# Half-filled products of w1's last 64 rows, in pairs on the two row halves of TensorE

## The chip, the cores and the metric

The kernel runs on one core of a Trainium2 chip. The metric is device time in microseconds for one launch, from the start to the end of the program on that core. A change of about 0.5% (6 us) can be told from no change.

## What is computed

A dynamic convolution feeds a two-level mixture of experts. For each of 23040 tokens (8 sequences of 2880) with 192 channels in 8 heads, seven softmax weights mix the token and the six before it. The result goes to one of 16 experts: the best of 4 groups, then the best of 4 experts in that group.

```python
w = softmax(weight_gen)                     # 8 heads, 7 taps a token
x = sum_k w[..., k] * x_shifted[k]          # 192 channels
g = argmax(x @ w_group); e = argmax(x @ w_expert[g])
h = maximum(x @ w1[g, e], 0)                # 192 -> 1024
out = p(g) * p(e) * (h @ w2[g, e])          # 1024 -> 192
```

All inputs and the output are fp32.

## The kernel before

**Stages.** VectorE computes the convolution for 15 groups of tokens, each group 12 tokens for each of the 128 partitions, in two chunks of 6. TensorE transposes and scores a group (`logits`, with `score` on four tiles of 32 columns, line 375). VectorE ranks the tokens (`ranks`) and writes a list of row numbers (`posi`, line 489), and GpSimd scatters the group's twelve columns of rows by it into `rows` in DRAM, sorted by expert (`scatter_row`, line 503). After certain groups `table` makes a table of the blocks of rows that are full. Such a set of blocks is a round. Round 5 takes the tokens up to group 6.

**Visits.** A visit takes one block of 128, 256 or 384 tokens of one expert through both products. The order of the visits is fixed by `ROUNDS`: round 0 has ten visits of 128, rounds 1 to 11 have 4, 5, 7, 5, 7, 5, 6, 7, 5, 4 and 5 visits of 256 (round 10 starts with one of 384), and rounds 12 and 13 the rest. In this text visit k is the k-th, from 0, of those behind the ten short ones, so visit 9 is the first of round 3 and visit 21 the first of round 5. For rounds below 12, and short blocks, w2 is used in whole fp32 (`whole`), and these are the whole visits.

**First product (`gemm1`, line 907).** A whole visit of 256 has four units `u` of two 128-column tiles `v` of w1. The fp32 values are split in two parts each. `wa[:, 0]` and `wa[:, 1]` are the high and the low part of w1's first 128 rows. `wa[:, 2]` holds the high part of its last 64 rows on partitions 0 to 63, and their low part (`w1lo`) on 64 to 127. `xh` and `xl` are the high and low part of the tokens, with the last 64 channels standing on both halves. Five products of 128x256 make one column tile:

```python
terms = ((wa[:, 0, :], xh[:, 0, :]), (wa[:, 1, :], xh[:, 0, :]), (wa[:, 0, :], xl[:, 0, :]), (wa[:, 2, :], xh[:, 1, :]), (wa[:, 2, :], xl[:, 1, :]))
```

In the fifth only the high half of the weights counts; the other half multiplies low part by low part. The result stands in one of three banks `ph0` to `ph2`, taken in turn; ScalarE applies the Relu (line 913).

**Second product (`gemm2`, line 945).** It runs two units behind the first, adds up the eight tiles into `py0` and `py1`, one bank for each 128 tokens, and ScalarE copies them to `y` (line 954, `finish`), from which GpSimd stores them by token number (line 962, `send`). The tokens of a visit are loaded by SyncE (line 779, `xb`), copied by ScalarE (`xd`, line 865), and transposed on TensorE (`tpx`, lines 881 and 882) behind the second unit of the visit before; VectorE makes `xl` from it (line 840, through `delay`).

**Order.** TensorE, ScalarE, VectorE and SyncE execute in the order in which the code is written by a planner: `run` adds up assumed costs for each engine in `clk`, and `fill` puts front work (convolution, softmax, ranking, tables) on VectorE until its clock reaches TensorE's. `gemm1` of a whole unit counts 1.09 us, `gemm2` 1.28. `pump` writes the loads. GpSimd's order is chosen by the compiler. A load of a round's tokens waits for the scatters of all groups up to that round's last.

## Time and profile before

| | us |
|---|---|
| median of three timed runs | 1199.54 (1197.88 to 1202.95) |
| profiled execution, its own time | 1193.24 |
| its span | 1191.6 |
| TensorE busy in it | 1132.8 |
| VectorE busy in it | 959.7 |

The profile is one execution of its own; differences are worked out against its 1193.24 and then moved to the median. Start times in the timelines are microseconds from the start of the span. Lengths of products on TensorE are modelled and overlap, so the distance from one start to the next is what a product takes in a row.

### The profile page before, as it was taken

What the parts mean: (1) busy time and instruction counts of PE and PEld (TensorE: products, weight loads), DVE (VectorE), ACT (ScalarE), POOL (GpSimd) and SP (SyncE); (2) the same over time, 40 slices, a digit from 0 to 9 for tenths busy, and PEclk for the clock granted to TensorE, in tenths of its full rate; (3) what the DMA queues carried; (4) which work ended last, traced back from release to release, by engine and by line L of the source; (5) the groups of instructions that cost most, each with busy time, mean ns of one, the idle gap of its engine ahead of it and who ended that gap; (6) DMA issues with size and microseconds to landing.
All of it is one profiled execution on the core that took longest, in us unless ns stands there. A gap on an engine that the chain in (4) does not pass through costs nothing.

```text
span 1191.6 us, 24474 instructions
## 1 busy us (share of the span) xinstructions
PE 1132.8 (95%) x8357; PEld 1073.7 (90%) x8357; DVE 959.7 (81%) x1646; ACT 651.2 (55%) x1235; POOL 569.1 (48%) x608
## 2 busy tenths in 40 slices
PE   5787899999999999999999999999999989999998
PEld 3444788999999999999999999999899989999997
DVE  8899898999998999899999999898535756666661
ACT  1331345565565655655655655655556766666572
POOL 6154183756273747575656555374664112222211
PEclk9997999999999999999999999999999999999999
DMA  5698799887888877888687878558688675555562
GB/s 172 212 308 224 264 303 308 267 266 249 255 253 261 282 221 239 274 253 264 211 298 228 281 223 293 186 160 257 203 271 256 217 196 159 160 161 159 164 200 76
DMA packets 82758, 275.08 MB, mean 231 GB/s; under 512 B 15063, under 2 KB 31734, under 8 KB 80832
## 3 DMA queue, kind: packets, MB, share of 16 engines
q1 hardware_dynamic: 62296, 229.76, 61.9%
q0 software_dynamic: 20208, 43.39, 11.5%
q8 instruction: 67, 1.10, 0.4%
q14 instruction: 67, 0.55, 0.2%
q10 hardware_dynamic: 120, 0.28, 0.1%
HBM read 225.83 MB, written 48.42 MB: 230 GB/s over the span
## 4 chain that ended last, share of the span: by engine, by line
PE 58%; issue 20%; DVE 7%; DMA 6%; POOL 5%; SPq 2%; ACT 1%; POOLq 1%; DVEq 0%; ACTq 0%
PE py L945 26%; PE ph L907 24%; POOL out L962 4%; DVE pr L294 3%; PE pl L375 2%; DMA raw<-w1lo 1%; PE tpx L882 1%; DMA out<-y,xb 1%; PE tpx L881 1%; DMA wt<-in_weight_gen 1%; DMA w1lo<-raw 1%; DMA xb<-rows 1%; PE ph L335 1%; PE tp L392 1%; POOLq L557 1%
## 5 line engine op out<-in xcount | busy, mean ns | idle before, releaser
L907 PE MATMUL ph<-xh,wa 128*128 128x256 f32 (+1 forms) x1992 | 465.5, 307 | 0.0
L962 POOL DMA_INDIRECT out<-y,xb x189 | 204.9, 1084 | 438.7 <-DVE y L960 193.8
L945 PE MATMUL py<-wc,hh 128*128 128x192 f32 x2160 | 399.9, 326 | 2.1 <-ACT y L954 2.1
L907 PE MATMUL ph<-xl,wa 128*128 128x256 f32 (+1 forms) x1328 | 360.2, 290 | 0.3 <-DVE xl L840 0.3
L945 PEld LDWEIGHTS py<-wc,hh 128*128 128x128 f32 x2160 | 346.4, 190 | 2.4 <-ACT y L954 2.3
L907 PEld LDWEIGHTS ph<-xh,wa 128*128 128x128 f32 x1992 | 337.5, 190 | 3.3 <-issue 1.8
L913 ACT ACTIVATE hh<-ph 128x512 f32<-128x512 f32 (+2 forms) x296 | 165.5, 559 | 262.0 <-PE ph L907 261.8
L294 DVE TENSOR_TENSOR pr<-xin,wt 128x1152 f32<-128x1152 f32 x186 | 248.9, 1350 | 5.5 <-PE py L335 3.5
L907 PEld LDWEIGHTS ph<-xl,wa 128*128 128x128 f32 x1328 | 251.9, 190 | 0.6 <-DVE xl L840 0.6
L503 POOL DMA_INDIRECT rows<-xrow,ix x156 | 227.4, 1457 | 49.4 <-POOL ix L502 35.8
L312 DVE TENSOR_TENSOR xrow<-xrow,pr 128x1152 f32<-128x1152 f32 x144 | 194.6, 1351 | 0.7
L840 DVE SCALAR_TENSOR_TENSOR pr<-ph,hh 128x384 fp32r<-128x384 f32 (+1 forms) x128 | 77.5, 606 | 99.8 <-ACT hh L918 98.6
L840 DVE TENSOR_TENSOR wa<-raw,wa 128x1024 fp32r<-128x1024 f32 x83 | 101.4, 1222 | 31.1 <-ACT wa L816 30.9
L947 PE MATMUL py<-wc,hh 128*128 128x384 f32 x352 | 110.6, 362 | 0.0
L918 ACT ACTIVATE hh<-ph 128x384 fp32r<-128x384 f32 (+1 forms) x128 | 68.4, 534 | 69.8 <-PE ph L907 69.8
L502 POOL COPY ix<-posi 128x1 int32<-128x1 int32 x156 | 70.0, 458 | 63.7 <-DMA rows<-xrow,ix 36.2
L816 ACT CAST wa<-raw 128x1024 fp32r<-128x1024 f32 x83 | 87.2, 1050 | 3.1 <-DMA raw<-in_moe_w 3.1
L948 PE MATMUL py<-wc,pr 128*128 128x192 f32 x352 | 88.0, 250 | 0.0
L825 ACT CAST wa<-raw 128x1024 fp32r<-128x1024 f32 x83 | 86.7, 1045 | 0.6 <-DMA raw<-w1lo 0.6
L954 ACT ACTIVATE y<-py,xb 128x192 f32<-128x192 f32 x179 | 67.1, 422 | 21.4 <-PE py L945 19.7
L840 DVE TENSOR_TENSOR xl<-tpx,xh 128x512 fp32r<-128x512 f32 (+1 forms) x94 | 61.5, 655 | 17.0 <-ACT xh L887 16.2
L948 PEld LDWEIGHTS py<-wc,pr 128*128 128x128 f32 x352 | 67.1, 191 | 0.0
(178 smaller groups left out, 1341.8 us busy)
## 6 DMA issues: line engine op xcount, KB each, us to landing
wc<-in_moe_w SPq DMA_DIRECT2D x73, 768.0 KB, 5.8
raw<-in_moe_w SPq DMA_DIRECT2D x83, 512.0 KB, 5.4
xin<-in_x SPq DMA_DIRECT2D x14, 1728.0 KB, 10.0
raw<-in_moe_w SPq DMA_DIRECT2D x91, 256.0 KB, 5.2
raw<-w1lo SPq DMA_DIRECT2D x83, 256.0 KB, 5.4
raw<-in_moe_w SPq DMA_DIRECT2D x22, 768.0 KB, 6.8
xb<-rows SPq DMA_DIRECT2D x72, 194.0 KB, 3.8
wa<-in_moe_w SPq DMA_DIRECT2D x24, 384.0 KB, 5.0
```

Of the source, the lines that this page charges most:

```text
L294: nc.vector.tensor_tensor(out=dst, in0=o.xin[:, c0 + k:c0 + k + SC, :].rearrange("p s (h g) -> p s h g", g=HG), in1=w4[:, c0:c0 + SC, :, k ...
L312: nc.vector.tensor_tensor(out=acc, in0=acc, in1=prs[k - 2], op=ALU.add)
L503: written_once(nc.gpsimd.indirect_dma_start(out=rows[:, :], out_offset=bass.IndirectOffsetOnAxis(ap=ix, axis=0), in_=src, in_offset=None, ...
L816: nc.scalar.copy(out=o.wa[:, 0, :], in_=o.raw[0])
L825: nc.scalar.copy(out=o.wa[:, 2, :], in_=o.raw[1])
L840: f(*a, **k)
L907: nc.tensor.matmul(ph[:, v, :], lhsT=w[:, f0:f0 + P], rhs=rhs, start=i == 0, stop=i == len(terms) - 1)
L913: nc.scalar.activation(out=hh, in_=ph, func=AF.Relu)
L945: nc.tensor.matmul(b.acc[t], lhsT=hh[:, v, c], rhs=wc[0][:, f, :], start=f == 0 and not (b.wide and t == 1), stop=f == NFT - 1 and not (b. ...
L947: nc.tensor.matmul(b.py[t], lhsT=hh[:, v, c], rhs=wc[f // 4][:, f % 4].rearrange("p l d -> p (l d)"), start=f == 0, stop=False)
L948: nc.tensor.matmul(b.acc[t], lhsT=hl[:, v, c], rhs=wc[f // 4][:, f % 4, 0, :], start=False, stop=f == NFT - 1)
L962: ins = nc.gpsimd.indirect_dma_start(out=out[:, :], out_offset=bass.IndirectOffsetOnAxis(ap=b.x.bitcast(I32)[:, t, D + 1:D + 2], axis=0), ...
```

## The change

The fifth product is taken out of the whole visits of 256 tokens (`shares`) wherever the visit before is of 128 tokens or such a visit too (`paired`). In its place stand eight products on 64 rows at the head of the visit, with the high weights and the low tokens alone: the one of unit 0 on rows 0 to 63 and the one of unit 1 on rows 64 to 127, and so on, in four pairs. For this, half of the columns have their high part on partitions 64 to 127: the last 64 rows are loaded by four DMAs instead of two, and w1's column tiles are put in another order on the host, which `column` undoes. The head writes to four banks at once, so the fourth unit uses `py1`, and the two outputs of these visits share `py0`. The planner's costs for a unit are 0.88, with 0.6 more for the head.

```diff
--- before.py
+++ after.py
@@ -795,8 +795,11 @@
                 for _ in q[0]:
                     pass
             slow.clear()
-            for h, src in enumerate((w1v[bass.ds(o.ev, 1), P:D, :], w1lo[bass.ds(o.ev, 1), :, :])):
-                nc.sync.dma_start(out=o.raw[1][h * HP:(h + 1) * HP, :], in_=src.rearrange("o p f -> p (o f)"))
+            for c in range(2):
+                cols = slice(c * F // 2, (c + 1) * F // 2)
+                for h, src in enumerate((w1v[bass.ds(o.ev, 1), P:D, cols], w1lo[bass.ds(o.ev, 1), :, cols])):
+                    q = (h + c) % 2
+                    nc.sync.dma_start(out=o.raw[1][q * HP:(q + 1) * HP, cols], in_=src.rearrange("o p f -> p (o f)"))
         else:
             if o.whole:
                 o.wc = [wp.tile([P, NFT, D], F32, name="wc", bufs=4)]
@@ -891,10 +894,45 @@
 
     relus = [0.0] * 3
 
+    def column(f):
+        a, c, v = f // 4, f // 2 % 2, f % 2
+        return c * (F // 2) + (2 * a + v) * P
+
+    def shares(n):
+        return whole(n) and order[n][1] == 2
+
+    def gemm1_paired(b, u):
+        wa, xh, xl = b.o.wa, b.xh[:, :, 0:b.n], b.xl[:, :, 0:b.n]
+        cost = 0.88
+        if u == 0:
+            b.ph = [ph_tile(k, [P, 2, BK]) for k in range(3)] + [ps_y.tile([P, 2, BK], F32, name="py1")]
+            for k in range(0, NU, 2):
+                for v in range(2):
+                    for h in range(2):
+                        r = slice(h * HP, (h + 1) * HP)
+                        f0 = column(2 * (k + h) + v)
+                        nc.tensor.matmul(b.ph[k + h][:, v, :], lhsT=wa[r, 2, f0:f0 + P], rhs=xl[r, 1, :], start=v == 0, stop=False, skip_group_check=True)
+            cost += 0.6
+        ph = b.ph[u]
+        terms = ((wa[:, 0, :], xh[:, 0, :]), (wa[:, 1, :], xh[:, 0, :]), (wa[:, 0, :], xl[:, 0, :]), (wa[:, 2, :], xh[:, 1, :]))
+        for v in range(2):
+            f0 = column(2 * u + v)
+            for i, (w, rhs) in enumerate(terms):
+                nc.tensor.matmul(ph[:, v, :], lhsT=w[:, f0:f0 + P], rhs=rhs, start=False, stop=i == len(terms) - 1, skip_group_check=True)
+        t = run("pe", cost, b.txh, b.txl, b.o.tw, relus[-3])
+        relus.append(run("act", 0.5, t))
+        b.th[u] = relus[-1]
+        hh = wp.tile([P, 2, BK], F32, name="hh", bufs=3)
+        b.h[u] = (hh, None)
+        nc.scalar.activation(out=hh, in_=ph, func=AF.Relu)
+
     def gemm1(b, u):
         while b.o.pending:
             flush()
         wa = b.o.wa
+        if b.paired:
+            gemm1_paired(b, u)
+            return
         if b.plain:
             terms = tuple((wa[0:DC, t, :], b.xh[:, t, :]) for t in range(2))
         else:
@@ -902,7 +940,7 @@
             terms = ((wa[:, 0, :], xh[:, 0, :]), (wa[:, 1, :], xh[:, 0, :]), (wa[:, 0, :], xl[:, 0, :]), (wa[:, 2, :], xh[:, 1, :]), (wa[:, 2, :], xl[:, 1, :]))
         ph = shaped(next_ph(), b)
         for v in range(b.nv):
-            f0 = (b.nv * u + v) * P
+            f0 = column(b.nv * u + v)
             for i, (w, rhs) in enumerate(terms):
                 nc.tensor.matmul(ph[:, v, :], lhsT=w[:, f0:f0 + P], rhs=rhs, start=i == 0, stop=i == len(terms) - 1)
         t = run("pe", 0.86 if b.plain else 0.82 if b.wide else 1.09, b.txh, b.txl, b.o.tw, relus[-3])
@@ -927,7 +965,10 @@
 
     def gemm2(b, u):
         wc = b.o.wc
-        if u == 0:
+        if u == 0 and b.shares:
+            py = ps_y.tile([P, 2 * D], F32, name="py0")
+            b.acc = [py[:, 0:D], py[:, D:2 * D]]
+        elif u == 0:
             b.py = [ps_y.tile([P, 2 * D], F32, name=f"py{t}") for t in range(min(2, b.nt))]
             b.acc = [py[:, 0:D] for py in b.py]
             if b.wide and b.o.whole:
@@ -942,7 +983,8 @@
             for t in range(b.nt):
                 c = slice(t * P, (t + 1) * P)
                 if b.o.whole:
-                    nc.tensor.matmul(b.acc[t], lhsT=hh[:, v, c], rhs=wc[0][:, f, :], start=f == 0 and not (b.wide and t == 1), stop=f == NFT - 1 and not (b.wide and t == 0))
+                    shared = b.wide or b.shares
+                    nc.tensor.matmul(b.acc[t], lhsT=hh[:, v, c], rhs=wc[0][:, f, :], start=f == 0 and not (shared and t == 1), stop=f == NFT - 1 and not (shared and t == 0))
                     continue
                 nc.tensor.matmul(b.py[t], lhsT=hh[:, v, c], rhs=wc[f // 4][:, f % 4].rearrange("p l d -> p (l d)"), start=f == 0, stop=False)
                 nc.tensor.matmul(b.acc[t], lhsT=hl[:, v, c], rhs=wc[f // 4][:, f % 4, 0, :], start=False, stop=f == NFT - 1)
@@ -1042,6 +1084,8 @@
             b.clears = n == nmain - 4
+            b.shares = shares(n)
+            b.paired = b.shares and (n == n0 or plain(n - 1) or shares(n - 1))
             if not b.plain:
...
+        if name == "moe_w1":
+
+            g, e, n, f = a.shape
+            a = a.reshape(g, e, n, 2, 2, f // 4).transpose(0, 1, 2, 4, 3, 5).reshape(g, e, n, f)
```

**TensorE, the head of visit 1.** Before, behind the three transposes of a score, in which `xh0`, `xl0` and `wa` are this visit's:

```order
L392 MATMUL tp_2281<-ident_105,xrow_1652 128x128 x2
L393 MATMUL tp_2281<-ident_105,rem_2267 128x128
L907 MATMUL ph0_2293<-xh0_177,wa_2003 128x256 x2
L907 MATMUL ph0_2293<-xl0_179,wa_2003 128x256
L907 MATMUL ph0_2293<-xh0_177,wa_2003 128x256
L907 MATMUL ph0_2293<-xl0_179,wa_2003 128x256
L907 MATMUL ph0_2293<-xh0_177,wa_2003 128x256 x2
L907 MATMUL ph0_2293<-xl0_179,wa_2003 128x256
L907 MATMUL ph0_2293<-xh0_177,wa_2003 128x256
L907 MATMUL ph0_2293<-xl0_179,wa_2003 128x256
L945 MATMUL py0_2231<-wc_1955,hh_2229 128x192
```

The same place now:

```order
L392 MATMUL tp_2288<-ident_105,xrow_1652 128x128 x2
L393 MATMUL tp_2288<-ident_105,rem_2274 128x128
L914 MATMUL ph0_2300<-xl0_179,wa_2009 128x256
L914 MATMUL ph1_2301<-xl0_179,wa_2009 128x256
L914 MATMUL ph0_2300<-xl0_179,wa_2009 128x256
L914 MATMUL ph1_2301<-xl0_179,wa_2009 128x256
L914 MATMUL ph2_2302<-xl0_179,wa_2009 128x256
L914 MATMUL py1_2303<-xl0_179,wa_2009 128x256
L914 MATMUL ph2_2302<-xl0_179,wa_2009 128x256
L914 MATMUL py1_2303<-xl0_179,wa_2009 128x256
L921 MATMUL ph0_2300<-xh0_177,wa_2009 128x256 x2
L921 MATMUL ph0_2300<-xl0_179,wa_2009 128x256
```

The two products with `xl0` and the last 64 rows of the first unit are gone from their places, as are those of the other three units, and eight products stand ahead of all others, to four banks; the second product behind them writes to one bank.

**VectorE, where group 6's scatter list is made.** Before, the list `posi` is followed by the `xl` of visit 17, the last row here:

```order
L483 TENSOR_TENSOR sel<-sel,oh 128x192
L486 TENSOR_REDUCE pos<-sel 128x12
L489 SCALAR_TENSOR_TENSOR posi<-pos 128x12
L294 TENSOR_TENSOR pr<-xin,wt 128x1152
L528 TENSOR_TENSOR units<-cnt,per_unit 128x16
L529 TENSOR_TENSOR units<-units,origin_163 128x16
L530 SCALAR_TENSOR_TENSOR units<-units,done 128x16
L840 TENSOR_TENSOR wa<-raw_189,wa 128x1024
L840 TENSOR_TENSOR xl_179<-tpx,xh_177 128x2x256
```

Now the `xl` in these rows is that of visit 18, and the list comes behind it:

```order
L475 SCALAR_TENSOR_TENSOR pre<-smask_152,pre 128x192
L480 TENSOR_TENSOR sel<-pre,pl 128x192
L481 TENSOR_TENSOR cnt<-pre,pl 128x16
L843 TENSOR_TENSOR wa<-raw_190,wa 128x1024
L843 TENSOR_TENSOR xl_180<-tpx,xh_178 128x2x256
L483 TENSOR_TENSOR sel<-sel,oh 128x192
L486 TENSOR_REDUCE pos<-sel 128x12
L489 SCALAR_TENSOR_TENSOR posi<-pos 128x12
```

In between, the `xl` of visit 17 and most of the ranking of the group have come ahead of visit 18's. The list has moved by one visit and a part of one.

**GpSimd, among the twelve scatters of group 6.** Before, the rows from the fourth scatter on (`ix` is a copy of a column of the list, `out_0` an output store):

```order
L502 COPY ix1_173<-posi_4724 128x1
L503 DMA rows_89<-xrow_3269,ix1_173 188928x194
L502 COPY ix2_174<-posi_4724 128x1
L503 DMA rows_89<-xrow_3269,ix2_174 188928x194
L502 COPY ix0_172<-posi_4724 128x1
L962 DMA out_0<-y1_182,xb1_170 23040x192
L503 DMA rows_89<-xrow_3269,ix0_172 188928x194
L962 DMA out_0<-y2_183,xb1_170 23040x192
L502 COPY ix1_173<-posi_4724 128x1
L503 DMA rows_89<-xrow_3270,ix1_173 188928x194
```

The same scatters now:

```order
L502 COPY ix1_173<-posi_4920 128x1
L503 DMA rows_89<-xrow_3408,ix1_173 188928x194
L502 COPY ix2_174<-posi_4920 128x1
L503 DMA rows_89<-xrow_3408,ix2_174 188928x194
L502 COPY ix0_172<-posi_4920 128x1
L503 DMA rows_89<-xrow_3408,ix0_172 188928x194
L502 COPY ix1_173<-posi_4920 128x1
L503 DMA rows_89<-xrow_3409,ix1_173 188928x194
L502 COPY ix2_174<-posi_4920 128x1
L503 DMA rows_89<-xrow_3409,ix2_174 188928x194
```

The two output stores of visit 15 are no longer in between. They and the two of visit 16 stand ahead of the first scatter now, where before the last stores ahead of it were those of visit 14.

## Rows read from the trace of the kernel before

**Rows 1.** the page, part 1: busy time, share of the span, instructions

```profile
PE 1132.8 (95%) x8357; PEld 1073.7 (90%) x8357; DVE 959.7 (81%) x1646; ACT 651.2 (55%) x1235; POOL 569.1 (48%) x608
```

**Rows 2.** windows: busy PE, PEld, DVE, ACT, POOL; clock; DMA share; GB/s

```profile
350.00:400.00 50.00, 50.00 (x405) 49.29 (x405) 45.33 (x84) 28.87 (x56) 26.51 (x27) 1.00 0.83 266
```

**Rows 3.** timeline, TensorE, in a visit: start us, us, engine line, matmuls, shapes, count

```profile
404.32 0.29 PE L907 MATMUL ph<-xl,wa 128*128 128x256 f32 x1
...
405.27 1.47 PE L945 MATMUL py<-wc,hh 128*128 128x192 f32 x8
...
406.58 0.38 PE L392 MATMUL tp<-ident,xrow 128*128 128x128 f32 x2
```

**Rows 4.** timeline, TensorE: four transposes and what follows them

```profile
410.60 0.27 PE L881 MATMUL tpx<-ident,xb 128*128 128x128 f32 x1
...
411.03 1.47 PE L945 MATMUL py<-wc,hh 128*128 128x192 f32 x8
```

**Rows 5.** timeline, TensorE, around a pass of column tiles (L375)

```profile
360.57 1.47 PE L945 MATMUL py<-wc,hh 128*128 128x192 f32 x8
...
361.96 1.52 PE L375 MATMUL pl<-xT,wr 128*32 128x128 f32 x48
...
363.75 0.28 PE L907 MATMUL ph<-xl,wa 128*128 128x256 f32 x1
```

**Rows 6.** timeline, TensorE's weight loads, the same place; in brackets the idle time before

```profile
361.96 1.25 PEld L375 LDWEIGHTS pl<-xT,wr 128*32 128x32 f32 x48 [0.23 <-issue]
363.41 0.30 PEld L907 LDWEIGHTS ph<-xh,wa 128*128 128x128 f32 x2 [0.20 <-issue]
```

**Rows 7.** timeline, ScalarE, around the head of a visit

```profile
405.54 0.60 ACT L913 ACTIVATE hh<-ph 128x512 f32<-128x512 f32 x1 [0.78 <-PE ph L907]
...
412.21 0.75 ACT L954 ACTIVATE y<-py,xb 128x192 f32<-128x192 f32 x2 [0.28 <-PE py L945]
```

**Rows 8.** timeline, TensorE: the second product after that store pair

```profile
413.52 1.47 PE L945 MATMUL py<-wc,hh 128*128 128x192 f32 x8
```

**Rows 9.** timeline, VectorE: scatter list of group 6, xl of visit 18

```profile
387.72 0.17 DVE L489 SCALAR_TENSOR_TENSOR posi<-pos 128x12 int32<-128x12 f32 x1
...
400.55 0.69 DVE L840 TENSOR_TENSOR xl<-tpx,xh 128x512 fp32r<-128x512 f32 x1
```

**Rows 10.** timeline, GpSimd: first and last of group 6's twelve scatters

```profile
389.59 0.98 POOL L503 DMA_INDIRECT rows<-xrow,ix  x1 [0.16 <-POOL ix L502]
...
419.31 1.80 POOL L503 DMA_INDIRECT rows<-xrow,ix  x1 [0.28 <-DMA raw<-in_moe_w]
```

**Rows 11.** timeline, SyncE: issue of w1 rows; load of visit 21's tokens

```profile
403.19 0.47 SPq L799 DMA_DIRECT2D raw<-w1lo  x1
...
422.66 0.35 SPq L779 DMA_DIRECT2D xb<-rows  x1
```

**Rows 12.** timeline, ScalarE: y of visits 3 and 16, xd of 9 and 21

```profile
254.38 0.75 ACT L954 ACTIVATE y<-py,xb 128x192 f32<-128x192 f32 x2 [0.28 <-PE py L945]
...
296.62 0.40 ACT L865 COPY xd<-xb 128x256 f32<-128x256 f32 x1
...
400.80 0.75 ACT L954 ACTIVATE y<-py,xb 128x192 f32<-128x192 f32 x2 [0.28 <-PE py L945]
...
432.63 0.40 ACT L865 COPY xd<-xb 128x256 f32<-128x256 f32 x1
```

**Rows 13.** timeline, TensorE: first transpose for visit 18, and for visit 21

```profile
399.18 0.27 PE L881 MATMUL tpx<-ident,xb 128*128 128x128 f32 x1
...
434.38 0.27 PE L881 MATMUL tpx<-ident,xb 128*128 128x128 f32 x1
```

**Rows 14.** the page, part 5: output stores on GpSimd, busy us, mean ns

```profile
L962 POOL DMA_INDIRECT out<-y,xb x189 | 204.9, 1084 | 438.7 <-DVE y L960 193.8
```

**Rows 15.** the page, part 6: DMA issues, count, size, us to landing

```profile
raw<-w1lo SPq DMA_DIRECT2D x83, 256.0 KB, 5.4
...
xb<-rows SPq DMA_DIRECT2D x72, 194.0 KB, 3.8
```

## Prediction

> **What bounds the kernel now.** I read the parts of the page first. TensorE is busy for 1132.8 of 1191.6 us, VectorE for 81% of the span [rows 1]. The table by stretches says where that average holds: in the middle TensorE is busy for all of 50 us, VectorE for 45.3, at granted clock 1.00 [rows 2]. So the bound there is the row of matrix products, with VectorE close behind, and the price of a product is the distance from one start to the next, since a record's own length overlaps its successors. In the timeline of TensorE eight products of 128x256 start between 404.32 and 405.27, 0.119 us each; the eight records of the second product (four products in two passes) fill the 1.31 us up to 406.58 [rows 3]. A visit of 256 tokens is then 4 x (10 x 0.119 + 1.31) plus four transposes, 0.43 [rows 4], 10.4 us.
>
> **The pairs.** 59 visits are paired: 4 + 5 + 7 + 5 + 7 + 5 + 6 + 7 + 5 + 4 + 5 = 60 of 256 tokens in rounds 1 to 11, less the one behind the 384-token visit. Each drops eight products, 8 x 0.119 = 0.953 us, and gains four pairs at its head. If the members of a pair run side by side, a pair costs what one product does, 0.119, so 0.476 for four. That is an estimate: no product on 64 rows stands in this trace.
>
> The array's shape has to change twice for it, to two tiles of 64 rows and back. The nearest thing in the trace is the scoring pass, which changes to four tiles of 32 columns and back. A second product begins at 360.57, so the next work was due at 361.88; the first weight load of the pass begins at 361.96, after an idle time of 0.23 on the weight-load row [rows 5, 6]. So 0.08 to 0.09 is lost before the load, and the load itself can't hide. A load of 128 columns takes 0.107, as the four transposes show, whose 128-column stream is short and which start 0.107 apart [rows 4]. Entry: 0.20. On the way back, the pass has 48 records in groups of four, 12 groups; I take 0.107 a group and 0.03 for the first load, so its streaming ends at 361.96 + 0.03 + 1.28 = 363.27. The third product behind it starts at 363.75 [rows 5], so the first was worth 363.75 - 0.24 = 363.51, and its load began at 363.41 after an idle 0.20 [rows 6]. Exit: 0.22 to 0.24. Sum for a visit: 0.20 + 0.476 + 0.22 - 0.953 = -0.06 us; times 59 is **-3.5 us**. The two changes of shape eat nearly all that the pairs win. Bounds: no price for them, 59 x -0.476 = -28; members that take turns, 59 x (0.20 + 0.953 + 0.22 - 0.953) = +25. I take the column rows' price, the only change of shape that the trace has.
>
> **What else is cheap.** The head needs `py1` free, which the last Relu of the visit before reads. That Relu runs from 405.54 to 406.14 [rows 7]; the head could begin at 406.58 and touches `py1` some 0.4 later: no wait. Both outputs of a visit now share one bank, so the next second product waits for both copies. They end at 412.96 [rows 7] and it starts at 413.52 [rows 8]; the first product ahead of it is two products, 0.24, shorter, so 0.32 of 0.56 is left: no wait. If that cover went, each 0.1 us would cost 59 x 0.1 = 6 us. The last 64 rows come by four DMAs instead of two: two more issues of 0.47 on SyncE for each visit [rows 11], the same bytes, landing after 5.4 [rows 15], asked for about one visit ahead: no cost.
>
> **The planner.** This is the part that costs. The planner now thinks that a visit is 4 x 0.21 - 0.6 = 0.24 shorter, and TensorE's true gain is 0.06, so it puts less of VectorE's front work beside each visit. Where the order of VectorE is shown, group 6's scatter list stands ahead of visit 17's xl before, and behind visit 18's xl now. Round 5, whose first visit is 21, can't load its tokens until group 6's twelve scatters have landed. VectorE runs in order, and visit 18's xl waits for TensorE, so the list can't be earlier than that place.
>
> Worked on the timeline of before: visit 18's xl starts at 400.55 [rows 9], so the list, three short operations on, is there at about 402, against 387.72. GpSimd's order has the output stores of visit 16 ahead of the scatters now; their copies end at 401.55 [rows 12], two stores of 1.08 [rows 14] end at 403.7, and the first scatter follows after 1.9, as it followed the list before (387.72 to 389.59) [rows 9, 10]: 405.6. From first to last took 29.7 [rows 10], with two stores in between; now none stand there, so 27.2 to 29.7, and I take 27.6: 433.2. From the last scatter to the load's issue took 3.35 (419.31 to 422.66) [rows 10, 11], and the load lands after 3.8 [rows 15]: 440.4. TensorE's transposes of visit 21 stood at 434.38 [rows 13]; between visit 18's transposes and these the changed order has one scoring pass (363.51 - 361.88 = 1.63, by rows 5) and six transposes (0.64 by rows 4) fewer, and three pairs' gains, 0.2, so they are due at 431.9. **TensorE waits 8.5 us**, and everything behind it on SyncE and ScalarE waits along. The bounds are 6.5 and 11: two us either way for the scatters, and half a us for the outputs' copies, which come late after it. Nothing gives this back, since from there to the end TensorE is the bound. The next tightest is round 3: visit 3's copies end at 255.13, and 38.9 later (as 401.55 to 440.4) is 294.0, before visit 9's token copy at 296.62 [rows 12]. No wait there; 0 to 2 us in the range. The later rounds have more room.
>
> **Sum.** -3.5 + 8.5 = +5.0 us. The profiled execution took 1193.2, so it would take 1198.2. The three timed runs have a median of 1199.5, 6.3 above it, so I forecast **1204.5**. With the wait's bounds and 0.1 us either way in a visit's pairs, this case runs from 1197 to 1213; with both at their likely values, 1200 to 1209.
>
> **The rivals.**
> *The change of shape is nearly free.* For it: the column pass loads its weights into new tiles with 48 records in 1.45 us, so tiles overlap well, and a 64-row tile lies in the same columns as before, so its loads might hide. Against it: both idle times in rows 6. Gain 0.25 to 0.476 a visit, -15 to -28, and +8.5: 1180 to 1193. The Trainium skill, "TensorEngine Tiling (Array Packing)", § Theoretical Speedup, promises up to a factor of 2 for a dimension of at most 64; by it alone the pairs give the full -28 of this case. No run so far shows it.
> *The pairs don't overlap their loads: the slower side.* If the weight load of a row half can't pass the product still running on that half, a pair costs 0.107 + 0.119 = 0.226, and a visit 0.09 + 4 x 0.226 + 0.22 - 0.953 = +0.26: +15 us and the wait, 1223. If the members take turns, +25 and the wait, 1233. It decides as soon as a pair costs over 0.15 us. Against it: the column pass hides its loads behind the group before. The Trainium skill, "TensorE: Matmul & The Clock Gate", § The mechanism, says that a weight load overlaps running products only where the row groups differ; by it the first of these holds, 1223. The rows speak against so strict a rule: whole-array products at 0.119 hide loads of 0.107 in the same rows [rows 3, 4].
> *The wait doesn't come.* If the scatters or the list are earlier than I think, the pairs alone are left: 1196. Against it: an order fixed in the program.
>
> **How the numbers follow.** About 0.5% (6 us) is what a measurement can tell from no change. Forecast 0.42: half of it within, nearly half slower, as it lies at the border. Free change of shape 0.25: four fifths faster, else within. Loads that don't overlap 0.25: slower. No wait 0.08: within. Faster 0.20, within 0.05 + 0.22 + 0.08 = 0.35, slower 0.20 + 0.25 = 0.45. The range takes in most of the rivals: 1186 leaves out half of the free change, 1232 only members that take turns.
>
> **What would show it.** Pairs: the starts of the new 64-row products, two together and 0.12 from pair to pair, and idle times of about 0.2 on the weight-load row at both ends of the head. A head of 0.9 us from the second product to the first whole product is right; 0.5 means that the change of shape is free, 1.2 or more that loads or members don't overlap. The wait: one gap of 7 to 11 us on TensorE ahead of visit 21's transposes, near 430 us, released by the token load, with SyncE's load waiting for a scatter, and no such gap elsewhere. Wrong would be: no gap there, waits for the output copies at each visit, or the heads at another price.

## The result and the profile after

The changed kernel has a median of 1217.60 us (1214.63 to 1219.26, four runs) against 1198.71 (1197.64 to 1202.95, four runs) of the kernel before beside it: ratio 1.0148, interval 1.0115 to 1.0181. It is slower by 18.9 us, as forecast in sign, but by 13.1 us more than the 1204.5 that was forecast.

The profiled execution has a span of 1215.1 us, 23.5 above that of before. Part 1 of its page shows TensorE busy for 8.5 us more and its weight loads for 14 us less than in [rows 1]:

```profile
PE 1141.3 (94%) x8357; PEld 1059.7 (87%) x8357; DVE 960.2 (79%) x1646; ACT 648.2 (53%) x1235; POOL 582.9 (48%) x608
```

**Where the time went.** Each visit of 256 tokens has one copy `xh` on ScalarE, so its starts tell how late each visit is. Visit 0 is already 6.1 us late; that is not the change (see the run of before once more). From there, after less before, less these 6.1: visit 20 at -1.4 us, visit 22 at +8.8, visit 53 at +5.0, visit 56 at +16.1, the last visit at +17.4. So there are two steps, of 10.2 and 11.1 us, and between them 3.8 us come back. At both steps TensorE waits for tokens. The timeline of TensorE (start, length, engine, line, operation; in brackets the idle time before and what ended it):

```profile
437.96 0.28 PE L921 MATMUL ph<-xh,wa 128*128 128x256 f32 x1
445.29 0.47 PE L884 MATMUL tpx<-ident,xb 128*128 128x128 f32 x1 [7.05 <-DMA xb<-rows]
...
446.43 2.59 PE L987 MATMUL py<-wc,hh 128*128 128x192 f32 x8
448.86 0.38 PE L392 MATMUL pl<-ident,xrow 128*128 128x128 f32 x2
...
829.23 0.48 PE L884 MATMUL tpx<-ident,xb 128*128 128x128 f32 x1 [5.81 <-DMA xb<-rows]
```

The first is the forecast one, ahead of visit 21 (7.05 us, where 8.5 was forecast). Behind it a second product takes 448.86 - 446.43 = 2.43 us in place of the 1.31 of [rows 3]. The table of stretches (busy us of PE, PEld, DVE, ACT, POOL; granted clock; DMA share; GB/s) shows why: the granted clock fell within the wait (0.84 from 435 to 445), and behind it part of the work ran at the lower level, 1.2 GHz (0.63 from 445 to 450).

```profile
425.00:435.00 10.00, 10.00 (x78) 9.63 (x77) 9.73 (x9) 6.77 (x14) 7.23 (x7) 1.00 0.99 328
435.00:445.00 10.00, 3.24 (x25) 3.02 (x23) 9.93 (x10) 0.60 (x1) 8.14 (x8) 0.84 0.58 200
445.00:450.00 5.00, 4.71 (x22) 4.43 (x23) 2.74 (x3) 3.65 (x8) 1.62 (x3) 0.63 0.91 275
450.00:460.00 10.00, 10.00 (x113) 9.25 (x112) 7.80 (x15) 5.54 (x11) 1.70 (x2) 1.00 0.60 205
```

The second wait was not forecast. It belongs to visit 54, the third behind the visit of 384 tokens (visit 51). Its tokens go to the same tile `xb` as that visit's, so their load has to wait until GpSimd has stored the three outputs of visit 51, whose token numbers stand in that tile. (A visit of 256 tokens fills two of the tile's four blocks, the first two and the last two by turns. The visit of 384 fills three, so it is in the way of the next visit on that tile.) GpSimd's timeline, then SyncE's, then what SyncE's load waited for from 795 to 830 (us in total, times, longest):

```profile
820.05 0.97 POOL L503 DMA_INDIRECT rows<-xrow,ix  x1 [0.30 <-issue]
821.33 0.97 POOL L1004 DMA_INDIRECT out<-y,xb  x1 [0.30 <-issue]
822.60 1.07 POOL L1004 DMA_INDIRECT out<-y,xb  x1 [0.31 <-issue]
823.98 0.97 POOL L1004 DMA_INDIRECT out<-y,xb  x1 [0.30 <-issue]
```

```profile
798.34 0.47 SPq L802 DMA_DIRECT2D raw<-w1lo  x1
826.84 0.34 SPq L779 DMA_DIRECT2D xb<-rows  x1
```

```profile
SPq L779 <- DMA out<-y,xb: 26.8, 1, 26.8
```

The three stores stand behind group 12's scatters in GpSimd's queue. SyncE is held from 798.8 to 826.84, and goes on 2.9 us after the last store's start. In the changed order of VectorE the lists of just two groups have moved by two copies `xl`: group 6's (17 `xl` ahead of it before, 19 now) and group 12's (51, now 53; both of these belong to visit 51, which has two). The others have moved by one at most.

**The head.** TensorE around the head of a visit, then its weight loads:

```profile
410.29 1.47 PE L987 MATMUL py<-wc,hh 128*128 128x192 f32 x8
411.68 0.62 PE L914 MATMUL ph<-xl,wa 64*128 64x256 f32 x5
412.03 0.28 PE L914 MATMUL py<-xl,wa 64*128 64x256 f32 x1
412.14 0.28 PE L914 MATMUL ph<-xl,wa 64*128 64x256 f32 x1
412.14 0.28 PE L914 MATMUL py<-xl,wa 64*128 64x256 f32 x1
412.35 0.50 PE L921 MATMUL ph<-xh,wa 128*128 128x256 f32 x2
412.69 0.28 PE L921 MATMUL ph<-xl,wa 128*128 128x256 f32 x1
```

```profile
411.68 0.41 PEld L914 LDWEIGHTS ph<-xl,wa 64*128 64x128 f32 x5 [0.23 <-DVE own L576]
...
412.03 0.18 PEld L914 LDWEIGHTS py<-xl,wa 64*128 64x128 f32 x1
412.35 0.30 PEld L921 LDWEIGHTS ph<-xh,wa 128*128 128x128 f32 x2
```

The members of a pair start together (412.14 twice), and from the second pair on the pairs are 0.11 to 0.12 apart (the third at 412.03, the fourth at 412.14). The loads wait 0.23 at the entry, as in [rows 6]; at the exit they wait 0.14 (from 412.03 + 0.18 to 412.35), where about 0.2 was forecast. From the second product's start to the third whole product behind it takes 412.69 - 410.29 = 2.40 us here, and 1.54 in the trace of before, where no head lies between. So the head is 0.86 us long where 0.896 was forecast, and 0.09 shorter than the eight products (0.953) that it replaces.

**The output copies.** In visits without scoring work the gain doesn't arrive: from visit 10's transposes to visit 11's TensorE takes 10.41 us before, and 10.45 or 10.46 in such visits now. ScalarE's copies of an output, as those at 412.21 in [rows 7] before:

```profile
407.14 0.73 ACT L996 ACTIVATE y<-py,xb 128x192 f32<-128x192 f32 x2 [0.60 <-PE py L987]
```

The last second product of that visit starts at 405.64, so the first copy comes 1.50 us behind it; before, it was 412.21 - 411.03 = 1.18 [rows 4, 7]. This holds at all visits of both traces where ScalarE is free (1.17 to 1.18, 1.50 to 1.51).

### The profile page after: what moved, and what is told of

Same layout as the page of the kernel before. It is cut to its first block, busy times and chain, and to the rows that moved or that the text cites. A ratio compares the mean times of both kernels' runs of the same rounds, so it can differ in the third digit from the quotient of the medians.

```text
span 1215.1 us, 24995 instructions
## 1 busy us (share of the span) xinstructions
PE 1141.3 (94%) x8357; PEld 1059.7 (87%) x8357; DVE 960.2 (79%) x1646; ACT 648.2 (53%) x1235; POOL 582.9 (48%) x608
## 4 chain that ended last, share of the span: by engine, by line
PE 56%; issue 21%; DVE 8%; POOL 7%; DMA 5%; ACT 2%; POOLq 1%; SPq 0%; DVEq 0%; ACTq 0%
PE py L987 24%; PE ph L921 13%; POOL out L1004 4%; PE py L921 4%; DVE pr L294 3%; PE ph L945 3%; PE ph L914 3%; POOL rows L503 2%; PE pl L375 1%; DMA raw<-in_moe_w 1%; PE tpx L885 1%; PE tpx L884 1%; PE ph L335 1%; DMA wt<-in_weight_gen 1%; DMA out<-y,xb 1%
## 5 line engine op out<-in xcount | busy, mean ns | idle before, releaser
L1004 POOL DMA_INDIRECT out<-y,xb x189 | 219.3, 1160 | 464.0 <-ACT y L996 195.6
L987 PE MATMUL py<-wc,hh 128*128 128x192 f32 x2160 | 408.7, 331 | 2.6 <-ACT y L996 2.6
L987 PEld LDWEIGHTS py<-wc,hh 128*128 128x128 f32 x2160 | 350.5, 192 | 6.2 <-ACT y L996 3.0
L503 POOL DMA_INDIRECT rows<-xrow,ix x156 | 223.8, 1434 | 46.2 <-POOL ix L502 35.0
L921 PE MATMUL ph<-xh,wa 128*128 128x256 f32 x1062 | 219.3, 303 | 0.0
L927 ACT ACTIVATE hh<-ph 128x512 f32<-128x512 f32 x177 | 106.4, 601 | 144.8 <-PE ph L921 144.8
L921 PEld LDWEIGHTS ph<-xh,wa 128*128 128x128 f32 x1062 | 167.7, 191 | 8.9 <-issue 0.2
L945 PE MATMUL ph<-xh,wa 128*128 128x256 f32 (+1 forms) x576 | 144.7, 317 | 0.0
L945 PE MATMUL ph<-xl,wa 128*128 128x256 f32 (+1 forms) x384 | 114.8, 310 | 0.0
L921 PE MATMUL ph<-xl,wa 128*128 128x256 f32 x354 | 100.1, 283 | 0.0
L945 PEld LDWEIGHTS ph<-xh,wa 128*128 128x128 f32 x576 | 95.6, 191 | 0.0
```

The lines of the kernel that those rows point to most:

```text
L503: written_once(nc.gpsimd.indirect_dma_start(out=rows[:, :], out_offset=bass.IndirectOffsetOnAxis(ap=ix, axis=0), in_=src, in_offset=None, ...
L921: nc.tensor.matmul(ph[:, v, :], lhsT=w[:, f0:f0 + P], rhs=rhs, start=False, stop=i == len(terms) - 1, skip_group_check=True)
L927: nc.scalar.activation(out=hh, in_=ph, func=AF.Relu)
L945: nc.tensor.matmul(ph[:, v, :], lhsT=w[:, f0:f0 + P], rhs=rhs, start=i == 0, stop=i == len(terms) - 1)
L987: nc.tensor.matmul(b.acc[t], lhsT=hh[:, v, c], rhs=wc[0][:, f, :], start=f == 0 and not (shared and t == 1), stop=f == NFT - 1 and not (sh ...
L1004: ins = nc.gpsimd.indirect_dma_start(out=out[:, :], out_offset=bass.IndirectOffsetOnAxis(ap=b.x.bitcast(I32)[:, t, D + 1:D + 2], axis=0), ...
```

## The experiments

The kernel before, timed beside them, has a median of 1201 us beside runs 1 to 4, 1228 beside runs 5 to 11 and 1200 beside run 12. Traces of runs 5 to 11 have pauses in visits with scoring work: some that last 12.4 to 13.1 us in the first trace of before take up to 19.6 there. Ratios, with a 95% interval in brackets, are always to the kernel before timed beside the run; they differ by up to 0.002 from the quotient of the two medians. Prices of a visit are read from visits without scoring work, which agree to 0.01 us throughout: 10.40 to 10.41 in the traces of before and in that of run 8.

**1. The planner's old costs (`e1_old_costs`).**

```diff
-        cost = 0.88
+        cost = 1.09
...
-            cost += 0.6
+            cost += 0.0
```

> The changed kernel with the planner's old costs (1.09 for each unit, nothing more for the head), so that VectorE's order is that of the kernel before, row for row. Theory 'planner': both token waits of the changed kernel (7.05 us at visit 21, 5.81 us at the first visit of round 11, with the slow products behind them about 10 us each) come from the planner's lower costs alone. Then they are gone here and the time falls by about 20 us, from 1217.6 to about 1197. Rival 'pairs': the time is lost in the heads and the output copies, visit by visit, and the order hardly matters: 1210 to 1218, with waits of like size at other visits. If the first waits go and others come in their place, the trace shows where.

1200.08 against 1200.98: ratio 0.9994 (0.9975 to 1.0013). The 18.9 us are gone. Visit 21's transposes follow the last product at once (435.32, 435.45), and visit 54's wait is down to 0.78 us:

```profile
435.32 0.28 PE L921 MATMUL ph<-xh,wa 128*128 128x256 f32 x1
435.45 0.27 PE L884 MATMUL tpx<-ident,xb 128*128 128x128 f32 x1
...
810.69 0.33 PE L884 MATMUL tpx<-ident,xb 128*128 128x128 f32 x1 [0.78 <-DMA xb<-rows]
```

**2. The new costs alone (`e2_new_costs_only`).**

```diff
-        t = run("pe", 0.86 if b.plain else 0.82 if b.wide else 1.09, b.txh, b.txl, b.o.tw, relus[-3])
+        pairs = whole(b.at) and b.nt == 2 and (b.at == 0 or plain(b.at - 1) or (whole(b.at - 1) and order[b.at - 1][1] == 2))
+        t = run("pe", 0.86 if b.plain else 0.82 if b.wide else 0.88 + (0.6 if u == 0 else 0.0) if pairs else 1.09, b.txh, b.txl, b.o.tw, relus[-3])
```

> The kernel before with nothing of the change but the planner's new costs (0.88 for each unit of a paired visit and 0.6 for its first). VectorE's order is that of the changed kernel, row for row; the products, banks and loads are those of before. Theory 'planner': two token waits on TensorE, ahead of visit 21 and of the first visit of round 11, 6 to 8 us each, with slower products behind them: 1198.7 + about 20 = 1215 to 1220. Rival 'pairs': no such waits, 1197 to 1201.

1217.80: ratio 1.0139 (1.0116 to 1.0163), the whole loss without one pair. TensorE waits at the same two visits:

```profile
442.56 0.47 PE L881 MATMUL tpx<-ident,xb 128*128 128x128 f32 x1 [9.44 <-DMA xb<-rows]
...
829.35 0.48 PE L881 MATMUL tpx<-ident,xb 128*128 128x128 f32 x1 [6.94 <-DMA xb<-rows]
```

The two runs settle the theory "planner" from both sides. (These two expectations call the second visit the first of round 11; the order of the loads shows that it is visit 54, in round 10.)

**3. The outputs in turn (`e3_outputs_in_turn`),** with the old costs:

```diff
+        if b.shares and u == NU - 1:
+            steps.sort(key=lambda s: s[1])
```

> As the run with the old costs, and in a visit's last unit of the second product all of the first output's products come ahead of the second output's, so that its copy can start about 0.65 us earlier. In the changed kernel each second product's first load is about 0.14 us late behind the two copies from the shared bank. Theory 'shared bank': the 0.14 us of each of 59 visits go, 8 us less than with the old costs alone (about 1189 against 1197), and no idle time of the weight-load row on the copies is left. Rival: the copy in the middle of the bank's use holds TensorE up, or the 0.14 us aren't a wait for the copies: no difference, or 59 x 0.3 = 18 us more.

1201.92, ratio 1.0003 (0.9974 to 1.0032): no gain, and the run does not test the theory. With the first output's four products ahead, its copy still starts 528.93 - 527.42 = 1.51 us behind the second product's start. In the program the first copy waits for a count of TensorE's that only the bank's last product reaches, whatever the order; the second copy has no wait of its own for TensorE. That is the cause of the 0.32 us: one bank is one tile, and its first reader waits for its last writer.

**4. The kernel before once more (`e0_before_again`),** unchanged.

> The kernel before once more, unchanged, for a second trace. In the changed kernel's trace visit 0 stands 7.0 us later than in the trace of before; of these about 2 us follow an idle time of 3.02 us at 141.84 (1.80 before) and about 3 us one of 2.56 us at 196.72 (2.13 before), each with a lower granted clock behind it. Theory 'chance': such falls of the clock in the first 200 us come and go from run to run, and this trace has some as well: visit 0 later than 197.45 by 2 us or more, total about 1199. Theory 'four loads': they come only with the four loads of the last rows, and visit 0 stands at 197 to 198 here, total about 1193.

1203.27 us, span 1201.7. Visit 0's `xh` stands at 205.99, against 198.96 in the first trace of before and 205.09 in the changed kernel's. The waits in the stage of short visits are long here too:

```profile
141.73 0.24 PE L459 MATMUL pl<-oh,tri 128*128 128x192 bf16 x1 [3.02 <-DVE oh L449]
...
197.65 1.65 PE L945 MATMUL py<-wc,hh 128*128 128x192 f32 x4 [3.60 <-ACT y L954]
```

So the early 6.1 us come without the change too: they are chance. From visit 10 to visit 56 this trace repeats the first one to 0.02 us, so differences of 0.05 us a visit between kernels can be read.

These traces side by side: start of `xh`, less that of before's first trace, from visit 0 on, in us:

| visit | after | new costs alone | old costs | before again |
|---|---|---|---|---|
| 20 | -1.4 | -1.1 | +1.1 | +1.9 |
| 22 | +8.8 | +12.3 | +1.0 | +1.9 |
| 52 | +6.4 | +11.3 | -0.3 | +1.9 |
| 53 | +5.0 | +9.6 | -0.1 | +1.9 |
| 56 | +16.1 | +21.1 | +1.5 | +1.9 |
| last | +17.4 | +24.2 | +7.1 | +2.9 |

With the old costs, visits 22 to 52 gain 1.3 us, 0.04 a visit: the pairs' 0.09 less the copies' wait where nothing hides it. Visit 54 and the last rounds give it back, with waits of 1.96 us for tokens at 914 and 1.91 for ScalarE at 926; the cause of these two was not tried, and before's second trace loses 1.1 us there as well.

**5. One bank for the outputs, alone (`e4_one_bank_only`).** The kernel before with

```diff
+        if u == 0 and b.shares:
+            py = ps_y.tile([P, 2 * D], F32, name="py0")
+            b.acc = [py[:, 0:D], py[:, D:2 * D]]
```

> The kernel before with nothing of the change but the outputs of whole visits in one bank, py0. In the traces the first output's copy starts 1.18 us after the start of the last unit's second product before, and 1.50 us with the shared bank, so the copies end 0.32 us later. Of the 0.56 us of room that the kernel before has, this leaves 0.24 less the way from the copy to TensorE (0.16, as the changed kernel's 2.41 - 2.25 show). Theory 'both together': with ten products between the two second products there is still no wait; a visit without scoring work stays at 10.40 us, as before, and the time at about 1201. It is only with eight products that the room is gone. Rival: the bank alone costs the 0.145 us; 10.55 us a visit and about 1207.

The visit stays at 10.41 (323.62 to 334.03, below): the bank alone is free, and only with eight products is the room gone. The whole kernel came out at a ratio of 1.0086 (1.0034 to 1.0138), which these visits don't explain. In its trace the surplus stands in visits with pauses; whether the bank has a part in them is not shown and stays open.

```profile
323.62 0.27 PE L881 MATMUL tpx<-ident,xb 128*128 128x128 f32 x1
...
334.03 0.27 PE L881 MATMUL tpx<-ident,xb 128*128 128x128 f32 x1
```

**6. The second product four products later (`e5_later_second`),** with the old costs:

```diff
+            if v == 0 and between:
+                between()
...
+                if u == 3 and cur.paired:
+                    between = lambda a=queue.pop(0): gemm2(*a)
```

> The changed kernel with the planner's old costs, and unit 0's second product put between the two column tiles of unit 3, four products (0.476 us) later; VectorE's, ScalarE's and GpSimd's orders are as with the old costs. Theory 'wait for the copies': a visit without scoring work falls from 10.455 us (10.405 before) to 10.31, the head's gain alone (0.095), and the time from 1200 by 59 x 0.05 to 0.145, 3 to 8 us, to about 1194, if the last rounds don't wait longer for their tokens. Rival: the 0.145 us isn't the copies: no difference to the old costs, 1200.

The visit falls to 10.30, as expected: the 0.15 us are the copies.

```profile
322.69 0.27 PE L884 MATMUL tpx<-ident,xb 128*128 128x128 f32 x1
...
332.99 0.27 PE L884 MATMUL tpx<-ident,xb 128*128 128x128 f32 x1
```

But the kernel has 1231.38 against 1227.93, ratio 1.0023 (0.9998 to 1.0048). Visits with scoring work that took 11.44 take 12.53, since the scoring transposes now stand right behind the first product and wait for ScalarE:

```profile
556.28 0.33 PE L393 MATMUL pl<-ident,rem 128*128 128x128 f32 x1 [1.00 <-ACT rem L385]
```

**7. Whole products at the head (`e6_whole_head`),** with the old costs. The head adds low part by low part too, as before.

```diff
-                        r = slice(h * HP, (h + 1) * HP)
...
-                        nc.tensor.matmul(b.ph[k + h][:, v, :], lhsT=wa[r, 2, f0:f0 + P], rhs=xl[r, 1, :], start=v == 0, stop=False, skip_group_check=True)
+                        nc.tensor.matmul(b.ph[k + h][:, v, :], lhsT=wa[:, 2, f0:f0 + P], rhs=xl[:, 1, :], start=v == 0, stop=False, skip_group_check=True)
```

> The changed kernel with the planner's old costs, and at the head eight products over all 128 rows in place of four pairs on 64 rows (as in the kernel before, low part by low part is added too). It has no change of the array's shape. If the head of four pairs costs 0.86 us (four pairs at 0.119 and 0.38 for two changes of shape), a visit without scoring work rises from 10.455 to 10.55 us (8 x 0.119 = 0.953 in place of 0.86). If the changes of shape were nearly free and the 0.86 us were something else that stays, a wait for xl say, it would rise by up to 0.48, to 10.93.

10.54 and 10.55 us a visit: 0.09 more than with pairs. The head's price as read from the trace is right. (One execution, 1248.47 us.)

```profile
323.00 0.27 PE L884 MATMUL tpx<-ident,xb 128*128 128x128 f32 x1
...
333.54 0.27 PE L884 MATMUL tpx<-ident,xb 128*128 128x128 f32 x1
```

**8. Four loads alone (`e7_four_loads`).** The kernel before with the last 64 rows loaded by halves of the columns:

```diff
+            for c in range(2):
+                cols = slice(c * F // 2, (c + 1) * F // 2)
```

> The kernel before with nothing of the change but the four loads of the last 64 rows, by halves of the columns, in place of two. Theory 'loads cost late': with the old costs the changed kernel still lost 3 to 7 us in the last rounds, where GpSimd's scatters wait for scatters before them; smaller packets on a full DMA would do that: waits of 1 to 3 us on TensorE from round 11 on, 1203 to 1206. Rival 'loads are free': as the kernel before, 1199 to 1202, visits as before to 0.01 us.

1230.09 against 1227.93, ratio 0.9996 (0.9961 to 1.0031), visits at 10.40 and 10.41. The loads are free within 0.4%; the rival of that expectation holds.

**9. The pairs twice (`e8_pairs_twice`),** with the old costs:

```diff
-            for k in range(0, NU, 2):
+            for k in (0, 2, 0, 2):
```

> The changed kernel with the planner's old costs, and each head's four pairs issued twice (the first four are overwritten by the second). A head of 0.86 us is, by the prediction, four pairs at 0.119 and two changes of shape, 0.38. Then four more pairs with no further change of shape cost 0.476: a visit without scoring work rises from 10.455 to 10.93 us. If the members of a pair took turns, it would be 0.95, to 11.41; if the head were mostly the price of pairs (0.2 each) and the changes of shape nearly free, about 0.8, to 11.25.

10.93 us a visit, 0.48 more: 0.12 for a pair. So of the head's 0.86 us the four pairs are 0.48, and the two changes of shape 0.38. (One execution, 1258.78 us.)

```profile
326.48 0.27 PE L884 MATMUL tpx<-ident,xb 128*128 128x128 f32 x1
...
337.41 0.27 PE L884 MATMUL tpx<-ident,xb 128*128 128x128 f32 x1
```

**10. Run 6 once more (`e9_later_second_again`),** the same kernel.

> The same kernel as the run with unit 0's second product four products later, timed in more rounds, since the chip it ran on took 1228 us for the kernel before, with pauses that no engine's work explains. Visits without scoring work at 10.30 us, 0.10 less than before. Theory 'heads win once the copies are covered': 59 x 0.05 to 0.10 = 3 to 6 us less than before, ratio 0.995 to 0.997. Rival 'the last rounds take it back': from round 11 on the tokens come no earlier, since VectorE and GpSimd set their time; then the gain of the visits ahead of round 11 is waited off there, ratio 0.998 to 1.002, with waits of 2 to 6 us for xb from visit 54 on.

Ratio 1.0009 (0.9980 to 1.0039). The visits with scoring work again have pauses. Neither theory holds: visits without scoring work are at 10.30 again, no wait for tokens of 0.9 us or more stands from visit 54 to the last rounds, but the visits with scoring transposes take 12.53 and up to 13.4 us where the old costs have 11.44, as in run 6.

**11. Higher costs (`e10_higher_costs`).** Run 6 with

```diff
-        cost = 1.09
+        cost = 1.17
```

> As the run with unit 0's second product later, with the planner's cost of a unit at 1.17 in place of 1.09, so that it plans 0.32 us more for a visit and puts VectorE's front work earlier: the lists of groups 7 to 14 stand one to three visits earlier. Theory 'order sets the token waits': the waits for xb from round 11 on go or shrink by 2 to 5 us, and the time is 1 to 5 us below that of the old costs with the later second product. Rival 'VectorE has no room': the work put ahead makes xl late, TensorE waits for VectorE at each visit up to 0.3 us, 5 to 15 us slower.

1239.31, ratio 1.0108 (1.0079 to 1.0136). Neither theory: VectorE's order can be too early as well. Group 13's scatters now stand ahead of visit 51's stores, and TensorE waits 13.30 us for a copy on ScalarE, which stands behind that of visit 54's tokens:

```profile
836.36 0.98 POOL L503 DMA_INDIRECT rows<-xrow,ix  x1 [0.28 <-POOL ix L502]
...
840.19 0.97 POOL L1009 DMA_INDIRECT out<-y,xb  x1 [0.31 <-issue]
```

```profile
842.67 0.34 SPq L779 DMA_DIRECT2D xb<-rows  x1
```

The load again follows the third store, by 2.5 us. It is the same place from the other side, and agrees with how the second wait comes about.

**12. Later where it is free (`e11_later_if_free`).** Run 6, with the second product kept ahead of scoring work:

```diff
+    def due():
+        while held2:
+            held2.pop(0)()
...
+            due()
             for u in range(2):
                 nc.tensor.transpose(out=tp[:, u, :], in_=row[:, u, 0:P], identity=ident)
```

> As the run with unit 0's second product four products later, but where scoring work is written between, the second product stays ahead of it as with the old costs. In that run some 14 visits with scoring transposes took 12.53 us in place of 11.44 and the like, since the transposes came to stand right behind the first product and waited 1.00 us for ScalarE's copy of rem; that alone is 14 to 16 us and took back the gain. Expected: visits without scoring work 10.30 us, as there; those of 12.53 back to 11.3 to 11.45; in sum 59 visits gain 0.09 on the mean against the kernel before, 5 to 6 us, ratio 0.993 to 0.997 if the token waits from round 11 on don't grow. Rival 'the last rounds take it back': 0.998 to 1.002.

1200.40 against 1199.80, ratio 1.0002 (0.9979 to 1.0025). The visits did what they should: 10.30 to 10.33 without scoring work, and by visit 52 the trace is 3.4 us ahead of before's, counted from visit 0. Then visit 54 takes all of it back:

```profile
815.15 0.47 PE L894 MATMUL tpx<-ident,xb 128*128 128x128 f32 x1 [3.54 <-DMA xb<-rows]
```

At visit 56 it stands at +2.4 us, 5.8 us lost around one wait of 3.54 (granted clock 0.66 from 815 to 820), and at the last visit at +6.0. No version in this study beats the kernel before.

## Why the prediction was right, and where it was not

The time fell into the range for a reason that is in part luck. The measured 1217.6 lies above the 1213 with which the prediction bounded its own case. It lies between 1186 and 1232 because the range also left room for pairs that do not overlap their loads (1223), and run 9 shows that they do overlap them.

**The pairs: right.** Members side by side, 0.12 a pair, and a price for two changes of shape (0.38; forecast 0.42, taken from the column pass). A visit gains 0.09 where 0.06 was forecast. Both rivals about the pairs fall: free changes by run 7, members or loads in turn by run 9. The Trainium skill's "TensorEngine Tiling (Array Packing)", § Theoretical Speedup, gives up to a factor of 2: the products alone come to it (0.48 for 0.953), the head as a whole doesn't (0.86). The rule of the Trainium skill's "TensorE: Matmul & The Clock Gate", § The mechanism, that a load overlaps only products in other row groups, would have given 0.226 a pair; run 9 measured 0.12.

**The output copies: wrong.** The step said that 0.32 of 0.56 us of room is left. It took the copies' end as it was. In one bank the first copy starts 0.32 later, and from the copies' end to TensorE it takes 0.16 (the copies end 2.24 us behind the start of the last second product, 1.50 + 0.74; the next second product is worth a start at 2.40). 0.56 - 0.24 - 0.32 - 0.16 = -0.16: the 0.15 us of run 6. Waits for the output copies at each visit are among the prediction's own signs of being wrong, and visits without scoring work have them. The text had priced it (0.1 us a visit is 6 us over 59 visits), but the rows needed, the first copy's start against the last product's, were there [rows 4, 7] and not used. In some visits with scoring work the wait is hidden (12.29 us with the old costs in place of 12.38), so pairs and copies together gave 0.04 a visit, near the 0.06 forecast, by two errors that cancel.

**`py1` and the four loads: right.** No head waits for the Relu; run 8 bounds the loads.

**The planner's wait at visit 21: right.** Counted from visit 18 (6.0 us late): list at 402.6 (forecast about 402), last scatter at 433.5 (433.2), from there to the load 3.29 (3.35), tokens at 439.3 (440.4), TensorE due at 432.2 (431.9). Wait 7.05 us, in the bounds 6.5 to 11. What the step left out is what a wait does to the products behind it: the step at visits 21 and 22 is 10.2 us in all, not 7.

**"The later rounds have more room": wrong, and the main miss.** The prediction gives no working for it. It looked at rounds 5 and 3 alone, and there at the first visit, and put everything behind at nothing; its sign "no such gap elsewhere" failed. Group 12's list moved as far as group 6's, to a place just as tight. The trace of before shows that there was no room: visit 54's load is issued at 806.89, 3.1 us after the last store of visit 51, and its second transpose stands 0.33 us behind its first where 0.11 is usual [rows 4]. SyncE's load already waits 21.4 us for the stores there (from 780 to 815; us in total, times, longest), ahead of TensorE's timeline:

```profile
SPq L779 <- DMA out<-y,xb: 21.4, 1, 21.4
```

```profile
809.30 0.27 PE L881 MATMUL tpx<-ident,xb 128*128 128x128 f32 x1
809.63 0.33 PE L882 MATMUL tpx<-ident,xd 128*128 128x128 f32 x1
```

**The sum.** Forecast -3.5 + 8.5 = +5.0. Measured, from visit 0: -1.4 up to visit 20, +10.2 at visit 21, -3.8 to visit 53 (among it scoring work that moved), +11.1 at visits 54 to 56, +1.3 behind them: +17.4, near the medians' 18.9. Run 2, with the same order and no pairs, has -1.1 and -2.7 at the first and the third place, so the pairs' own part up to visit 53 is about -1.4. Of the 12.4 us between +17.4 and the forecast +5.0, 11.1 are visits 54 to 56 and 1.7 visit 21: the slow products behind that wait took 3.1, and the wait was 1.5 shorter than forecast. The 6.3 us between the profiled execution of before and its median were rightly added: before's second trace is 10.1 us longer than its first, and 7.0 of these stand at visit 0.

## What to carry to other kernels

A planner's cost is an edit like any other: here 0.24 us less for a visit that became 0.04 shorter cost 17 us, seven times the 2.4 us (an estimate, 59 x the 0.04 of run 1) that the pairs win, and the same kernel with the old number is even with the one before. Where a new order moves several lists, follow each of them to the tile that its work frees, not only to the first reader of its data. And before you put two results into one bank, ask what the first reader will wait for: here it is the last writer of the bank.

## What the runs showed of the hardware

Two changes of the array between 128 rows and two tiles of 64 rows cost 0.38 us, as much as three pairs of 64x256 products; so eight half products in pairs save 0.09 us, not 0.48.

The granted clock fell in several waits of TensorE: behind 7.05 us it was 0.63 in the next 5 us and back at 1.00 by 450; behind 5.81 us it was 0.50 from 829 to 834; behind 3.54 us 0.66 from 815 to 820 (run 12). But the length of a wait alone does not tell whether it falls. In the trace of before, waits of 1.80 and 2.13 us left it at 1.00, and so did one of 3.44:

```profile
140.00:150.00 10.00, 8.94 (x70) 8.80 (x70) 9.52 (x40) 3.00 (x9) 4.82 (x7) 1.00 0.68 213
190.00:200.00 10.00, 7.76 (x58) 7.10 (x56) 7.18 (x30) 6.57 (x14) 4.31 (x7) 1.00 1.03 290
955.00:965.00 10.00, 6.56 (x45) 6.28 (x46) 5.28 (x8) 4.61 (x9) 1.51 (x2) 1.00 0.72 206
```

```profile
958.18 0.30 PE L881 MATMUL tpx<-ident,xb 128*128 128x128 f32 x1 [3.44 <-DVE xl L840]
```

In its second trace waits of 3.02 and 3.60 us at the first two of these places left 0.83 and 0.66 (means over 10 us):

```profile
140.00:150.00 10.00, 8.27 (x51) 8.11 (x51) 9.52 (x40) 2.11 (x6) 3.23 (x6) 0.83 0.38 117
195.00:205.00 10.00, 7.35 (x33) 7.35 (x34) 6.21 (x28) 4.55 (x10) 4.31 (x7) 0.66 1.05 292
```

And in run 1 a wait of 1.91 us left 0.66 in 5 us:

```profile
926.31 0.47 PE L885 MATMUL tpx<-ident,xd 128*128 128x128 f32 x1 [1.91 <-ACT xd L868]
```

```profile
925.00:930.00 5.00, 3.69 (x17) 3.70 (x18) 4.06 (x7) 4.26 (x9) 0.06 (x1) 0.66 0.42 115
```

What decides it is not shown here. Where the clock falls, a wait costs more than its length: 7.05 us became 10.2 at visit 21. Executions of one kernel differ in this, too: the two traces of before are 10.1 us apart, 7.0 of them by visit 0, where the waits of 3.02 and 3.60 us lie.

Last, the 1228 us of the kernel before beside runs 5 to 11 are not a matter of the chip alone: runs 9 to 11 (1228) and run 12 (1200) ran on chip number 6 alike. In run 8's trace, 26 of the 41 us that it takes longer than the first trace of before lie in eight visits with scoring work; what pauses there stays open.
